# Part of an output product multiplied in a job of its own, loads paced earlier, and a new written-out order, in a fused attention and maxout kernel

## The chip, the cores and the metric

The kernel runs on one core of a Trainium2 chip. The metric is device time in microseconds, from launch to the last store, median of several executions. Before the change it is 358.24 us (three runs: 357.92, 358.24, 360.69).

## The reference: what is computed

Attention with pooled queries (batch 8, 8 heads, 1152 keys, head size 64), then a maxout layer on its output. Cut to what matters:

```python
q_pool = q.reshape(B, H, S // 2, 2, D).mean(axis=3)          # 576 queries
scores = matmul(q_pool, k.transpose(0, 1, 3, 2)) / sqrt(D)
attn = exp(scores - max); attn /= sum(attn)
x = matmul(attn, v)  ->  (4608 tokens, 512 channels)
g = maximum(x @ w1, x @ w2)                                   # 1024 wide
out = g @ w_out                                               # (4608, 512)
```

## The kernel before

**The algebra.** The maximum is split: with wd = w1 - w2, g @ w_out = max(x @ wd, 0) @ w_out + x @ (w2 @ w_out). The product w2 @ w_out (called w21) is made once. So for each block of tokens there are two kinds of matmul jobs: an h job makes two of the eight feature tiles of max(x @ wd, 0) for one stretch of tokens (stretches in `HCUTS`), and a p job makes 256 tokens of the output from twelve contraction tiles: four channel tiles of x against w21 and eight feature tiles of g against w_out.

**Attention.** Heads are taken in 32 pairs, two heads in the two row halves of TensorE. The scores of a pair are 9 key tiles by 576 queries, laid out as one long row and cut into groups of 512 columns without regard to pair borders: 324 groups. A group is multiplied (L302, letter S), then ScalarE takes the exponential of 2 x 512 columns out of PSUM (L317, letter E; where the exponential buffer turns over a group is done in two, so there are 336 E). The exponentials are then weights of the product with v (L621 and L636, letter A), normalized on VectorE (letter a), transposed into the token-major xT (by DMA, letter x, or on TensorE, letter X) and used by h and p jobs.

**Feeding a pair.** Loads of q, k and v (letter l) go through SP's DMA queue. POOL pools and casts q (L435), casts k (L405) and v (L445); letters q, k, v. From pair 5 on k is transposed by a DMA (L475, letter t) and q by eight VectorE transposes of 32 partitions (L485, letter r). Scores of a pair need both.

**The order.** Nothing is scheduled at run time. A string is read letter by letter, and each letter appends one operation to its engine's queue. Every engine runs its queue in order and waits on semaphores for what it reads or overwrites; only the waits that are needed are emitted. The letters that matter here, beside those above: 0, 1, 2, 3 are four lanes in which jobs of the weights' kind are open (w makes w21, h and p as above; the order in which jobs are opened is the string `MOE`); each digit is one unit, two matmuls in the two row halves. 4, 5, 6, 7 empty the finished job of a lane on VectorE, 8, 9, + and - do so on ScalarE. d is a difference for wd, c a cast of a weight, o a store. `BANKS` says which of the eight PSUM banks each opened job or score group takes (a p job takes two, a "wide" bank). Counting the letters E ahead of a place gives its position in the stream of exponentials; positions in this document are such counts.

**The pace of loads.** A load is issued when its buffer is free and, from a certain E on, when the exponential two before the last one ordered so far has been done:

```python
def pace():
    g = done[0] - PACE
    return [f"E{g}"] if PACE and g >= PACE_FROM else []
```

Before that E the queue issues loads as soon as a buffer is free, ahead of the place of the letter.

**The output stage.** A finished p job is copied from PSUM into `osb2`, four rows of 512 values a partition, and stored from there. p job n uses rows 0 and 1 or 2 and 3, in turn.

Of the kernel before, what the change touches and what calls it, by code (L numbers as in the profile page):

```python
# [7 lines left out]
P = 128  # L8
# [4 lines left out]
ALU = mybir.AluOpType  # L13
# [103 lines left out]
def bass_funnel_attn__then__act_maxout2_kernel(  # L117
# [11 lines left out]
    E = moe_w_out.shape[1]  # L129
# [9 lines left out]
    NC_ = C // P  # L139
    NF = F // P  # L140
# [21 lines left out]
    FILL = 28  # L162
    FILLS = 16
    PACE = 2
    PACE_FROM = 40
    FOUR = 1
    LOADS = (
# [14 lines left out]
    )  # L182
    MOE = (
        "wwhhhhpphhhhpphhhhhhhhpphhhhpphhhhphhhhpphhhhphhhhphhhhpphhhhhhhhhphphh"
    )
    BANKS = (
        "0124605424023623462032424660232342630240624702402064202420472042646264246024604640164604264126402406"
        "0240260240246304260346204040640606062061262062062402740264062402406402640642704260202402402406401640"
        "6460462056204620462046042164206204620620426026402602602602604604614646046046024604604204620420642040"
        "6406406742064264264206520640260462620620162062046206240620206204230642042042424126426046046045620642"  # L190
        "6024062046206206206206412640246056046206404024024026423236042642042626260262626426454526420642064206"
        "2454"
    )

    ctx = ExitStack()
    with ctx:
# [51 lines left out]
        def rows(half):  # L248
            return slice(half * HP, half * HP + HP)
# [273 lines left out]
        def evac_op(eng, fn, r, w, cost, after=(), alt=None):  # L523
            return dict(eng=eng, fn=fn, r=r, w=w, cost=cost, after=after, alt=alt)
# [263 lines left out]
        def p_sides(j, n, z):  # L788
            if j < NC_:
                return xT[z, j, n:n + P], w21[z, j, :]  # L790
            c = n % RING
            return gT[z, j - NC_, c:c + P], wo[z, j - NC_, :]

        def p_job(n):
            lo = n * 2 * P
            o = n % 2 * 2

            def part(j, turn):
                def go(e, m):
                    for k in range(2):  # L800
                        z = rows(turn ^ k)
                        lhs, rhs = p_sides(j, lo + k * P, z)
                        last = e.matmul(fb[m + k][:, :], lhs, rhs, start=(turn == 0 and j == 0),  # L803
                                        stop=(turn == 1 and j == NC_ + NF - 1))
                    return last
                return p_reads(j, lo, lo + 2 * P), 0.216, "s", turn == 1 and j == 0, go

            def dve(e, m):
                return e.tensor_copy(osb2[:, o:o + 2, :], wide[m // 2][:, :, :])  # L809

            def act(e, m):
                return e.copy(osb2[:, o:o + 2, :], wide[m // 2][:, :, :])

            return Job(("p", n), 2, [part(j, turn) for turn in range(2) for j in range(NC_ + NF)],
                       [evac_op("DVE", dve, [], [f"osb{o}", f"osb{o + 1}"], 0.16 + 2 * E / 960.0,
                                alt=(act, 2 * E / 1200.0))])

        def spot(n):
            b, at = divmod(n, SQ)
# [73 lines left out]
        h_at, p_at, w_at = iter(hs), iter(ps), iter(ws)  # L893
        moe = [next({"h": h_at, "p": p_at, "w": w_at}[c]) for c in MOE]
        assert next(h_at, None) is None and next(p_at, None) is None
        dve_line = {"w": [lambda n=n: cast_k0(n) for n in range(len(K0_ENG)) if K0_ENG[n] == "DVE"],
                    "y": [lambda: cast_q0(0, 0, 4), lambda: cast_q0(0, 4, QU), lambda: cast_q0(1, 0, QU)],
# [59 lines left out]
                 "m": ("Z", 0), "4": ("0", 0), "5": ("1", 0), "6": ("2", 0), "7": ("3", 0),  # L957
                 "8": ("0", 1), "9": ("1", 1), "+": ("2", 1), "-": ("3", 1)}
        for c in (
            "luFFlulllfyKQklgfbSkKEFlgFKSgESyFFlKEFgQSbESlFkSFEFFKlEySFSgESlqFFEFQlSbEFkSQElbKvSEgSlESceAAEATcESA"  # L960
            "EAhlkSaSEaASclEKAEglSAEcSAElvSaTaEhElTcSAESlAhAEScAElSSAcEAAlAqESa0a00aE0la0ScAE0SldQEaa00bSd0lEXSj0"
            "00ESvTl0h0E00eS4SlEAAkAEAlSa1ad1E1S1SEl1q1S1E1Kl1g1qE1S1SE1lQkrAEbArSdtAErArSE11avlEa1S5AElSdArESSrA"
            "dArEArSAEkAlaAaSEaAdatAESaXadjXEjSjSEXq0jl00jE0S0qr0E0lSr01rE11e41Sl1E1Sk1r10Er005St0ESv00r0ESSr0rvE"
            "lA4AAEASqalSaEAArAErAlSrSEEaAeaAArxAErSSaAEaAklrAAErS1at1ak1E1r0Sr0xE0r0Sr11E1rS1r0E050Sl0E0q0SrS0tE"
            "r01r10Er0eS0r0E0r0Skr0lE0r1S0r0E0rlSv0r1E14S11El1S1oSE1oAAEASAkEAaAlaSAEtAvSa1aE1SxS11ES111E1111ES11"
            "l1ESq5AAEAlSrSoEAroArAESrkSArEAaAalAEAaAaSvaaEtaSSrXEqArAjAEAjSrle00Ea0aS0rSE0lr0vSr0E1r01rlE114S11E"
            "1S1rSEA5AlvAEASr0E0ta0Eva0SrSE00xe00SE4AAkAESSlAEAaAaAEAlSa1aE1Sx000E0Sk11E0lS11E11S50qlE00tS00ESer0"
            "0rSE00rS0rE00r00Er0l0qSrSE0r01l1r0E14S11E1l1SroSE1r1o11roSErAoArAtEkArAAaaAArq1ESaa1E1Sx001r001E1r0S"
            "1rE0l001rS141E1rS1r1ES5AAEvAAroSSrvoESAlAAEvAaAaAlEAaAkaSa000SaEt0a000011114Ee111S111115E1S111Xl5EvS"
            "j00j0ESl0qSE0000SEl4AAAEArSSaEAaArAlqEArS1a1taE11rSESrE1e1xrS1r1EA5AAEASla0kaE0Sr00rSEq0l0r0SEr0ArAl"  # L970
            "E4SAAESr11aE1a1Srx1ESr11r1SEt5qAAAEArSe0aE0a0Slr0SEkr0S0r0E0lrS0r0E0r0Sl0rE0000ES0S0Er0tArAEArArS0aE"
            "0aq0Srx10Er1S14k1E1S11EroS1rSo1E1oAAoEvAAS1vElSAAlEAvAaSa1ESalAaAAEASa1aE1taS1rXvE1rS1j11Ej1eSrl11rE"
            "11qrSS5EAlAAkEAroS0a0oEa0S0rS0ErAAlAEASa0a0E0l0S4x00E0qSE0r00E0trSA4eAEAArS1a1Ea1k1Sr11ESr1lSr1E5AAA"
            "lEArS1a1Ea11Srx00E10S1l1E1S500tE0Sq0rS0Er00r0e0ESr00rSEl0kr00r0E0rS0l0ES00SE0A4AAEAAaAoaAoASaoSqaE11"
            "x11SESkr11t1rE11rE11rE1SrS1E1r11r1SEr11S1E1S11E1A5AEvAASoSvESlAAoAEvAaAaAElAaAa0Sa0a0E0taS00r0000E04"
            "e0Sx000r0E11141vS1x1E11r100500Sr11qE1Sr01lr110E1rS050E0Sl0r0E0SS0l0E0S0r0EArAArEAArlAkaAaArSE0etEa0a"
            "S0r0SE0rxS0rq0EA4AAEASkao1aE11o1SSE11lS11EA5AAElASa1aE1Sx0r00E0rS1rt0E0er0Sr0E1S4111ESl1r0q0E500S0lE"
            "0SrS0r0EA4lAAEAAAaaAASa1aESlk1Sx1r1ES1r11Ert11r11Er1qSSr1E1rArAEvAS1E11klS11El11vS1E1S1lvA5ESAAEAoAa"
            "oSaSESaAtaArAEArq00Ea0aSa00rExSv0r00ErS0xe0r0E0rSSr0kl0E0S00E0Sl00E0S00El0A4AEAAAaoSaSEoArAtArE00Ea0"
            "0aeS00rxE1111r00qS411E1111151S1k1E1r1Sl00500ESr000SrEl0A4AAEArSla1aE1S1S1EAAAEAlSa1aE1tSrS1rq1E1r1x1"  # L980
            "1rESSre11Er11rSk1Elr11S1E11Sl1E1A5AAEASaoSaEAoAAoEAoSa0a0tEq00rSESr0E00rx00k040E0AArvAArSrSvElArArAE"
            "AvaAaAAaAaSaSaE00a001x14E11S11E1x11Sv511E100S1SE0r1t11r0ES0500E0eSr00Er00SrSE0r00r0SEr0S00E0S00E0004"
            "0E00S0E0oS00oSE4AAAEAAaAaAeAAaEAaAAxAaAaAASa0aES0x00SE1000E0S411E1S11E111500S0E00S11E1S11E1S10E50S00"
            "E0S10E0Se10E00S00E0S00E0S00E10S41E11S11EoS11o1E1oSSo1E1AAEAAAaAaAAAaAaAxAAAAAaAaAAaAa1a1a1a11X1j11j1"
            "11111900001111111150000111o080110091o110000008101110191101000018111009101110000080101111191100000001"
            "001111910000000011111111110001000800110000o008001o11o00010181111Z9ZZZZZoZZoZZZZZZmZZZZzzZZZZZZZZZZmZ"
            "ZZZZZZzZzmzz"
        ):
            step(c)
        plan.solve()  # L990
# [51 lines left out]
```

## Time and profile before

| what | value |
|---|---|
| median of three runs | 358.24 us (357.92 to 360.69) |
| profiled execution | 358.12 us, span 356.4 us |
| TensorE busy (modelled) | 346.0 us, 6178 matmuls |
| ScalarE busy | 313.8 us, of it exponentials 302.4 |
| VectorE busy | 230.1 us |
| POOL busy | 151.4 us |
| DMA queue of SP | 83.15 MB, 87.5% of 16 engines' span |
| HBM | 62.91 MB read, 9.44 MB written |
| granted TensorE clock | 0.999 |

How to read it: busy times are unions of the instructions' spans in one profiled execution. Matmuls are pipelined and their ends are modelled, so a TensorE that is shown busy may still be waiting within a run; its weight loads (PEld) show such waits better. Idle time in front of an instruction is given with what ended it. The chain that ended last is followed back from the last instruction. Idle time of an engine that isn't the bound costs nothing by itself.

### The profile page before, as it was taken

Reading aid. Unit: us, or ns where it says so; the run is one execution under the profiler, and the core shown is the slowest. Engines: PE = TensorE matmul, PEld = TensorE weight load, DVE = VectorE, ACT = ScalarE, POOL = GpSimd, SP = SyncE. Lnnn points to the kernel's source line nnn. Section 1 sums busy time; section 2 is a strip of 40 time slices with the busy share of each in tenths; the row PEclk is TensorE's granted clock in tenths of the full one; section 3 lists DMA queues with packets and bytes.
Section 4 is the critical chain, followed back from the end, with each engine's and each line's share of the span. In section 5 each row is a group of like instructions: output and inputs, shape, how many; then the busy total and the mean of one; then the engine's idle time right before and its main releaser. Section 6 shows DMA issues by size and latency. Waiting matters only on the chain.

```text
span 356.4 us, 13757 instructions
## 1 busy us (share of the span) xinstructions
PE 346.0 (97%) x6178; PEld 218.5 (61%) x6178; DVE 230.1 (65%) x472; ACT 313.8 (88%) x354; POOL 151.4 (42%) x136
## 2 busy tenths in 40 slices
PE   7889999999899999999999999999999999999996
PEld 5556665656564675656666576556576757448753
DVE  2587589974966867985887677785586875414001
ACT  5999999999999899999999989989999796992431
POOL 2625997554564264355544455227444621010000
PEclk9999999999999999999999999999999999999999
DMA  8999999999989989998999699998999943012215
GB/s 271 403 397 398 370 255 309 280 289 261 293 252 279 315 196 350 237 301 183 278 320 260 153 230 301 237 314 234 224 299 255 267 68 75 17 32 47 61 31 148
DMA packets 76699, 84.55 MB, mean 237 GB/s; under 512 B 48480, under 2 KB 49760, under 8 KB 76640
## 3 DMA queue, kind: packets, MB, share of 16 engines
q1 hardware_dynamic: 75856, 83.15, 87.5%
q8 instruction: 48, 0.79, 0.9%
q10 hardware_dynamic: 784, 0.52, 0.5%
q14 instruction: 11, 0.09, 0.1%
HBM read 62.91 MB, written 9.44 MB: 203 GB/s over the span
## 4 chain that ended last, share of the span: by engine, by line
PE 87%; ACT 9%; DMA 2%; issue 1%; SPq 0%; DVE 0%
PE ps L803 25%; PE ps L621 20%; PE ps L302 19%; PE ps L760 16%; ACT et L317 9%; PE ps L636 3%; PE ps L593 2%; DMA qraw<-in_q_dram 2%; PE ps L846 1%; PE ps L552 0%; PE ps L533 0%; SPq L346 0%; DVE qp L428 0%; SPq L358 0%; PE ps L730 0%
## 5 line engine op out<-in xcount | busy, mean ns | idle before, releaser
L317 ACT ACTIVATE et<-ps 128x1024 bf16<-128x1024 f32 (+1 forms) x336 | 302.4, 1019 | 14.5 <-PE ps L302 9.7
L302 PE MATMUL ps<-qpT,kT 64*128 64x256 bf16 (+7 forms) x1162 | 117.3, 283 | 2.7 <-issue 1.1
L485 DVE STREAM_TRANSPOSE qpT<-qp 32x288 bf16<-32x288 bf16 x216 | 101.4, 469 | 10.4 <-PE ps L302 6.1
L760 PE MATMUL ps<-xT,wd 64*128 64x512 bf16 (+3 forms) x832 | 81.2, 311 | 0.2
L302 PEld LDWEIGHTS ps<-qpT,kT 64*128 64x128 bf16 x1162 | 48.3, 94 | 49.7 <-ACT et L317 11.3
L803 PE MATMUL ps<-wo,stage 64*128 64x512 bf16 x544 | 76.4, 376 | 0.0
L435 POOL TENSOR_TENSOR qp<-qraw 128x576 bf16<-128x576 f32 x30 | 42.1, 1406 | 61.1 <-DMA qraw<-in_q_dram 57.3
L621 PEld LDWEIGHTS ps<-vE,et 128*128 128x128 bf16 x1728 | 54.9, 97 | 13.9 <-ACT et L317 9.3
L621 PE MATMUL ps<-vE,et 128*128 128x65 bf16 x1728 | 60.7, 193 | 0.7 <-issue 0.3
L771 DVE TENSOR_SCALAR stage<-ps 128x1024 bf16<-128x1024 f32 (+3 forms) x41 | 39.7, 970 | 21.1 <-PE ps L760 20.6
L760 PEld LDWEIGHTS ps<-xT,wd 64*128 64x128 bf16 x832 | 35.6, 94 | 22.2 <-PE ps L760 1.9
L405 POOL TENSOR_SCALAR kbf<-kraw 128x1152 bf16<-128x1152 f32 x31 | 35.7, 1153 | 26.3 <-DMA kraw<-in_k_dram 25.6
L803 PE MATMUL ps<-w,xT 64*128 64x512 bf16 x272 | 40.8, 377 | 0.0
L803 PEld LDWEIGHTS ps<-wo,stage 64*128 64x128 bf16 x544 | 26.4, 94 | 20.5
L445 POOL TENSOR_SCALAR vE<-vraw 128x1152 bf16<-128x1152 f32 x24 | 27.4, 1154 | 19.4 <-PE ps L636 10.8
L809 DVE COPY stage<-ps 128x1024 f32<-128x1024 f32 x14 | 17.1, 1224 | 23.1 <-PE ps L803 23.0
L468 POOL TENSOR_SCALAR stage<-et 128x1152 bf16<-128x1152 bf16 x14 | 16.1, 1152 | 35.5 <-ACT et L317 35.5
L654 DVE TENSOR_TENSOR xnat<-ps,rc 128x256 bf16<-128x256 f32 (+2 forms) x71 | 27.6, 397 | 2.0
L651 DVE RECIPROCAL rc<-ps 128x4 f32<-128x4 f32 (+2 forms) x64 | 11.6, 182 | 25.9 <-PE ps L621 25.5
L621 PEld LDWEIGHTS ps<-stage,et 128*128 128x128 bf16 x576 | 18.1, 97 | 2.7 <-issue 2.6
L621 PE MATMUL ps<-stage,et 128*128 128x65 bf16 x576 | 19.7, 193 | 0.0
L803 PEld LDWEIGHTS ps<-w,xT 64*128 64x128 bf16 x272 | 12.5, 94 | 8.8 <-DVE stage L771 0.2
(55 smaller groups left out, 155.4 us busy)
## 6 DMA issues: line engine op xcount, KB each, us to landing
vraw<-in_v_dram SPq DMA_DIRECT2D x32, 576.0 KB, 6.1
kraw<-in_k_dram SPq DMA_DIRECT2D x31, 576.0 KB, 6.7
qraw<-in_q_dram SPq DMA_DIRECT2D x31, 576.0 KB, 6.3
out_dram<-stage SPq DMA_DIRECT2D x24, 256.0 KB, 4.1
out_dram<-stage SPq DMA_DIRECT2D x21, 128.0 KB, 3.4
xT<-in_moe_w_dram SPq DMA_DIRECT2D x4, 512.0 KB, 12.2
stage<-in_moe_w_out_dram SPq DMA_DIRECT2D x4, 512.0 KB, 14.1
stage<-in_moe_w_dram SPq DMA_DIRECT2D x4, 512.0 KB, 13.2
```

The lines of the kernel that those rows point to most:

```text
L302: last = e.matmul(ps[:, h, col:col + hi - lo], kT[i % 3][rows(h), t, :], qpT[i % 3][rows(h), lo:hi], start=True, stop=True)
L317: op("ACT", lambda e: e.activation(et2[:, :, c:c + z - a], ps[:, :, a - g * W:z - g * W], EXP, scale=scale), r=[f"b{m}", f"b{m + 1}"], w=w ...
L405: op("POOL", lambda g: g.tensor_scalar(kbf[s][:, :, :, :].rearrange("p t h d -> p h t d"), kraw[r][:, :, :, :], 1.0, 1.0, ALU.mult, ALU.mu ...
L435: op("POOL", lambda g: g.tensor_tensor(qpf[s][:, :, :], qraw[r][:, :, 0, :], qraw[r][:, :, 1, :], ALU.add), r=[f"qraw{r}"], w=[f"qp{s}.0", ...
L445: return g.tensor_scalar(vE[r][:, :, :, 0:D].rearrange("p t h d -> p h t d"), vraw[s][:, :, :, :], 1.0, 1.0, ALU.mult, ALU.mult)
L485: op("DVE", lambda e: e.transpose(view[dst:dst + 32, :, 32 * pb:32 * pb + 32], qpf[s][src:src + 32, :, 32 * db:32 * db + 32]), r=[f"qp{s}. ...
L621: last = e.matmul(fb[m][:, at * 66:at * 66 + 65], et[:, a:a + P], vE[vs][:, t, half, 0:65], start=(t == 0), stop=(t == NT - 1))
L654: todo.append(evac_op("DVE", lambda e, m, z=z, at=at, num=num, dst=dst: e.tensor_tensor(dst, a(m)[z, at:at + num, 0:D], rc[k][z, at:at + n ...
L760: last = e.matmul(fb[m + k][:, 0:size], wd[z, ct, (f0 + k) * P:(f0 + k + 1) * P], xT[z, ct, n0:n1], start=(turn == 0 and ct == 0), stop=(t ...
L771: return e.tensor_scalar_max(gT[:, f0:f0 + 2, g0:g0 + size], wide[m // 2][:, :, 0:size], 0.0)
L803: last = e.matmul(fb[m + k][:, :], lhs, rhs, start=(turn == 0 and j == 0), stop=(turn == 1 and j == NC_ + NF - 1))
L809: return e.tensor_copy(osb2[:, o:o + 2, :], wide[m // 2][:, :, :])
```

## The change

Four things are edited.

1. A new kind of job, r (`pre_job`), for the first two p jobs (tokens 0 to 511): it multiplies the first `PRE = 2` of the twelve contraction tiles, both of them channel tiles, and its result is put into the rows of `osb2` which the p job will use. p jobs 0 and 1 then run over the other ten tiles, and their evacuation on VectorE adds the PSUM to what is in `osb2`. An r job is 4 units, and p jobs 0 and 1 have 20 units where they had 24.
2. `PACE_FROM` goes from 40 to 6, so loads are held to the pace from the ninth E on.
3. The sequence of `LOADS` is changed from q 7 on, and that of the differences for wd.
4. The order string, `MOE` and `BANKS` are new; jobs are spread over four lanes instead of two until late. The letters ahead of about 28 us are nearly the same.

The diff, with the long strings cut to the lines in which p jobs 0 and 1 stand:

```diff
-    W_DIFFS = ((3, 0), (3, 1), (1, 0), (2, 0), (2, 1), (0, 0), (0, 1), (1, 1))
+    W_DIFFS = ((2, 0), (1, 1), (2, 1), (1, 0), (0, 1), (3, 0), (0, 0), (3, 1))
...
-    PACE_FROM = 40
+    PACE_FROM = 6
...
-        ("k", 5), ("v", 3), ("w", 1, 0), ("k", 6), ("q", 6), ("q", 7), ("k", 7), ("v", 4), ("v", 5),
+        ("k", 5), ("v", 3), ("w", 1, 0), ("k", 6), ("q", 6), ("k", 7), ("q", 7), ("v", 4), ("v", 5),
...
-        ("v", 12), ("q", 13), ("v", 13), ("k", 15), ("q", 14), ("v", 14), ("k", 16), ("v", 15),
-        ("q", 15), ("q", 16), ("v", 16), ("q", 17), ("k", 17), ("v", 17), ("q", 18), ("k", 18),
...
+        ("q", 13), ("v", 12), ("q", 14), ("k", 15), ("k", 16), ("v", 13), ("q", 15), ("v", 14),
+        ("v", 15), ("k", 17), ("q", 16), ("q", 17), ("q", 18), ("k", 18), ("v", 16), ("v", 17),
...
     MOE = (
-        "wwhhhhpphhhhpphhhhhhhhpphhhhpphhhhphhhhpphhhhphhhhphhhhpphhhhhhhhhphphh"
+        "wwhhhhrprphhhhpphhhhhhhhpphhhhpphhhphhhhhpphhhhphhhhphhhphphhhhhhhhphhphh"
     )
+    PRE = 2
...
-        def p_job(n):
+        def pre_job(n):
+
             lo = n * 2 * P
             o = n % 2 * 2
 
...
                         last = e.matmul(fb[m + k][:, :], lhs, rhs, start=(turn == 0 and j == 0),
+                                        stop=(turn == 1 and j == PRE - 1))
+                    return last
+                return p_reads(j, lo, lo + 2 * P), 0.216, "s", turn == 1 and j == 0, go
+
+            def dve(e, m):
+                return e.tensor_copy(osb2[:, o:o + 2, :], wide[m // 2][:, :, :])
+
+            def act(e, m):
+                return e.copy(osb2[:, o:o + 2, :], wide[m // 2][:, :, :])
+
+            return Job(("r", n), 2, [part(j, turn) for turn in range(2) for j in range(PRE)],
+                       [evac_op("DVE", dve, [], [f"pre{n}"], 0.16 + 2 * E / 960.0,
+                                alt=(act, 2 * E / 1200.0))])
+
+        def p_job(n):
+            lo = n * 2 * P
+            o = n % 2 * 2
+            first_j = PRE if n < 2 else 0
+
...
             def dve(e, m):
+                if first_j:
+                    return e.tensor_tensor(osb2[:, o:o + 2, :], wide[m // 2][:, :, :], osb2[:, o:o + 2, :], ALU.add)
                 return e.tensor_copy(osb2[:, o:o + 2, :], wide[m // 2][:, :, :])
...
-            return Job(("p", n), 2, [part(j, turn) for turn in range(2) for j in range(NC_ + NF)],
-                       [evac_op("DVE", dve, [], [f"osb{o}", f"osb{o + 1}"], 0.16 + 2 * E / 960.0,
-                                alt=(act, 2 * E / 1200.0))])
+            return Job(("p", n), 2, [part(j, turn) for turn in range(2) for j in range(first_j, NC_ + NF)],
+                       [evac_op("DVE", dve, [f"pre{n}"] if first_j else [], [f"osb{o}", f"osb{o + 1}"],
+                                0.16 + 2 * E / 960.0, alt=None if first_j else (act, 2 * E / 1200.0))])
...
-            "lA4AAEASqalSaEAArAErAlSrSEEaAeaAArxAErSSaAEaAklrAAErS1at1ak1E1r0Sr0xE0r0Sr11E1rS1r0E050Sl0E0q0SrS0tE"
...
+            "AAAElArSrSEArAAaaAESaSaEltAEerAArAESqaSrAElrAAaAkESa1a11Er2t2rS2kE216S11E11qS53El33S33Er3SrS3E3r330E"
...
```

The rest of the order strings can't be shown at length; what the prediction says of places in them is counted from them letter by letter.

More of the change, by code (lines that the diff above doesn't have):

```diff
@@ L812, in act, with part, go @@
                 return e.copy(osb2[:, o:o + 2, :], wide[m // 2][:, :, :])
-            return Job(("p", n), 2, [part(j, turn) for turn in range(2) for j in range(NC_ + NF)],
-                       [evac_op("DVE", dve, [], [f"osb{o}", f"osb{o + 1}"], 0.16 + 2 * E / 960.0,
+            return Job(("r", n), 2, [part(j, turn) for turn in range(2) for j in range(PRE)],
+                       [evac_op("DVE", dve, [], [f"pre{n}"], 0.16 + 2 * E / 960.0,
                                 alt=(act, 2 * E / 1200.0))])
+        def p_job(n):
+            lo = n * 2 * P
+            o = n % 2 * 2
+            first_j = PRE if n < 2 else 0
+            def part(j, turn):
+                def go(e, m):
+                    for k in range(2):
+                        z = rows(turn ^ k)
+                        lhs, rhs = p_sides(j, lo + k * P, z)
+                        last = e.matmul(fb[m + k][:, :], lhs, rhs, start=(turn == 0 and j == first_j),
+                                        stop=(turn == 1 and j == NC_ + NF - 1))
+                    return last
+                return p_reads(j, lo, lo + 2 * P), 0.216, "s", turn == 1 and j == first_j, go
+            def dve(e, m):
[7 more added lines that the diff above has]
+                                0.16 + 2 * E / 960.0, alt=None if first_j else (act, 2 * E / 1200.0))])
         def spot(n):
@@ L892, in bass_funnel_attn__then__act_maxout2_kernel @@
         ws = [w_job(c) for c in W_PAIRS]
-        h_at, p_at, w_at = iter(hs), iter(ps), iter(ws)
-        moe = [next({"h": h_at, "p": p_at, "w": w_at}[c]) for c in MOE]
+        rs = [pre_job(n) for n in range(2 if PRE else 0)]
+        h_at, p_at, w_at, r_at = iter(hs), iter(ps), iter(ws), iter(rs)
+        moe = [next({"h": h_at, "p": p_at, "w": w_at, "r": r_at}[c]) for c in MOE]
         assert next(h_at, None) is None and next(p_at, None) is None
@@ L965, in bass_funnel_attn__then__act_maxout2_kernel @@
[L965 to L974, printed above, removed]
@@ L988, in bass_funnel_attn__then__act_maxout2_kernel @@
+            "AEAAaAaAeAAaEAaAkArArAAatAaSaSaE00ro00rSEo10rl00lEr0Sr1x1E41S11E1x13532S3xE33S22E2oS2o2E2oS2o3E633S3"
+            "E3S330E0eS33E3Sv33E30Sv3E3S333E3S700E00S0oE0S0o00EoSS00EAAAEAAaAaAAAaAaAxAAAAoAaAaAAaAa0a0a0a00X0j00"
+            "j0011118233331111222353332222o07000+111o103333000224221111005003333007022221+111332222018133222233+3"
+            "311-000000000001111222203222330030003111111103321+1111090307000oZ8ZoZZoZZoZZZoZZZZZZZmZZZZZzzZZZZZZZ"
+            "mZZZZZZZzZzmzz"
         ):
```

52 lines of the change are left out of this document (28 added, 24 removed), and 10 rows, old and new, of the table LOADS.

## The prediction

> **What bounds the kernel now.** I read the totals and the chain first, then the stages, then the groups and the waits of the engine that the stages point to.
>
> The page's totals and its chain that ended last:
>
> ```profile
> PE 346.0 (97%) x6178; PEld 218.5 (61%) x6178; DVE 230.1 (65%) x472; ACT 313.8 (88%) x354; POOL 151.4 (42%) x136
> PE 87%; ACT 9%; DMA 2%; issue 1%; SPq 0%; DVE 0%
> ```
>
> TensorE looks like the only bound. But a busy PE is modelled, so I cut the span where the work changes: start, the stretches that the chain gives to ScalarE, the body, and what follows the last exponential (stage, its length, then busy time of PE, PEld, DVE, ACT, POOL with counts, clock, DMA share, GB/s).
>
> ```profile
> 9.40:44.70 35.30, 32.49 (x686) 20.17 (x688) 24.00 (x40) 34.84 (x39) 22.03 (x20) 1.00 1.02 391
> 44.70:60.00 15.30, 14.89 (x254) 8.27 (x252) 13.38 (x29) 15.29 (x18) 14.02 (x12) 1.00 1.16 282
> 60.00:121.00 61.00, 59.74 (x1040) 37.35 (x1041) 45.40 (x95) 60.00 (x68) 31.41 (x27) 1.00 1.05 285
> 121.00:322.00 201.00, 200.72 (x3595) 126.23 (x3591) 139.54 (x288) 189.36 (x210) 82.14 (x69) 1.00 0.91 220
> 322.00:353.30 31.30, 31.23 (x524) 21.22 (x520) 4.74 (x15) 9.37 (x15) 0.00 (x0) 1.00 0.26 62
> 353.30:356.40 3.10, 0.00 (x0) 0.00 (x0) 0.26 (x1) 0.00 (x0) 0.00 (x0) 0.90 0.40 114
> ```
>
> Up to 121 us ScalarE is as full as TensorE; from 121 to 322 it idles 201.00 - 189.36 = 11.6 us; after 322 it has little to do and TensorE runs alone for 31.3 us, with 3.1 us of the last store behind it. So the time is a sum of three: the end of the exponentials (322.0), the TensorE tail (31.3), the store (3.1), together 356.4. The profiled execution took 358.12 us, 1.7 more than its span, and the median of the runs is 358.24; the sum is made against 358.12.
>
> The group of the exponentials, what ScalarE waited for in all, and two rows of its timeline:
>
> ```profile
> L317 ACT ACTIVATE et<-ps 128x1024 bf16<-128x1024 f32 (+1 forms) x336 | 302.4, 1019 | 14.5 <-PE ps L302 9.7
> ACT et L317 <- PE ps L302: 9.7, 15, 2.1
> ACT et L317 <- PE ps L621: 2.9, 3, 1.1
> 237.25 10.21 ACT L317 ACTIVATE et<-ps 128x1024 bf16<-128x1024 f32 x11 [1.07 <-PE ps L302]
> 314.46 7.51 ACT L317 ACTIVATE et<-ps 128x1024 bf16<-128x1024 f32 x8
> ```
>
> 302.4 us over 336 instructions is 0.90 us for one E of the order: that is the step in which I count below. The last E ends at 314.46 + 7.51 = 322.0. Idle before an E sums to 14.5 us, nearly all of it waiting for scores or for matmuls of L621. A change can thus gain by closing those waits, or by having less TensorE work behind the last E; it loses if scores come later.
>
> **The change part by part.** Positions are counted in the order strings of both kernels: the number of E ahead of a letter.
>
> *The work multiplied ahead.* Two r jobs of 8 matmuls (2 tiles x 2 turns x 2 blocks) leave p jobs 0 and 1, which lose 8 each. Rows for a run of 36 attention matmuls and one of eight of L803 (of the chain in order of time), the copy that empties p, and the stage in which p 0 and p 1 stand:
>
> ```profile
> 61.94 1.20 PE ps L621 x36
> 73.63 0.86 PE ps L803 x8
> L809 DVE COPY stage<-ps 128x1024 f32<-128x1024 f32 x14 | 17.1, 1224 | 23.1 <-PE ps L803 23.0
> 70.00:80.00 10.00, 10.00 (x129) 5.35 (x125) 7.84 (x14) 10.00 (x12) 5.68 (x5) 1.00 1.01 274
> 44.70 13.43 ACT et L317 x15
> ```
>
> The number of matmuls is the same: 2 x 0.86 = 1.7 us of TensorE is moved, not removed. It would be worth 1.7 us if it went where the chain runs through ScalarE (44.70 to 58.13, about steps 43 to 57), since TensorE has room there. In the new order it does not: r 0 stands at steps 69 to 70 with p 0 from 71, r 1 at 74 to 77 with p 1 from 79, while before p 0 began at 69 and p 1 at 74. It comes straight ahead of the job from which it was cut, in the same stretch. I counted every unit of TensorE ahead of each E, at 0.215 us for two matmuls of L803, L760 or a score group (less for narrower ones) and 0.30 for nine of L621, the same in both orders: from E 30 on they are never more than 0.45 us apart, equal at 221 of 306 places, and 31.9 against 31.6 us behind the last E, a shift that the body gets back as +0.3. So the move itself gives 0.
>
> It adds two evacuations of 1.22 us on VectorE, 2.45 us in a stretch where it is 7.84 of 10 us busy; the two p evacuations become additions of equal width. VectorE's room of 2.2 us there hides most. What waits behind: p 0 takes bank 2, which r 0 just filled, and stands only two score groups and five pairs of matmuls behind it, 7 x 0.215 = 1.5 us against an evacuation of 1.22. Between 0 and two whole evacuations (2.4 us), in the likeliest case covered; I take 0. Below nothing it can't go, since no work leaves.
>
> *ScalarE as evacuator.* The old order has no evacuation on ScalarE ahead of the last E; the new one has one, of h job (6, 6), at step 249. The copies to ScalarE behind the last E fall from 14 to 9, and VectorE, 4.74 of 31.3 us busy there, takes them. A whole-width evacuation of that kind is seen only as a copy:
>
> ```profile
> L812 ACT COPY stage<-ps 128x1024 f32<-128x1024 f32 x3 | 3.0, 1012 | 12.1 <-PE ps L803 12.1
> ```
>
> So up to 1.0 us in the stream of E. At this very place the row at 237.25 shows ScalarE waiting 1.07 us for scores (the E there has 249 others ahead of it). If the wait stays, the copy fills it: 0; if it goes, 1.0. I take +0.3.
>
> *Loads paced from E 6, not 40.* Until now the queue ran ahead (two issue groups with size and median landing, then the queue's and POOL's timeline, then a stage):
>
> ```profile
> stage<-in_moe_w_dram SPq DMA_DIRECT2D x4, 512.0 KB, 13.2
> qraw<-in_q_dram SPq DMA_DIRECT2D x31, 576.0 KB, 6.3
> 23.96 4.05 SPq L358 DMA_DIRECT2D qraw<-in_q_dram  x2
> 28.05 0.52 SPq L346 DMA_DIRECT2D kraw<-in_k_dram  x1
> 29.16 1.41 POOL L435 TENSOR_TENSOR qp<-qraw 128x576 bf16<-128x576 f32 x1 [4.35 <-DMA qraw<-in_q_dram]
> 31.79 2.49 POOL L506 TENSOR_TENSOR wd<-stage,xT 128x512 bf16<-128x512 f32 x2 [1.22 <-DMA stage<-in_moe_w_dram]
> 40.00:50.00 10.00, 9.99 (x224) 6.53 (x220) 7.49 (x16) 9.97 (x13) 10.00 (x10) 1.00 1.01 302
> ```
>
> The load of k 5 (letter at step 35) was issued at 28 us, when some 23 E were done. Under the new pace each load waits for an E two back, so 22 loads of about 0.55 MB go out over steps 9 to 40, 31 x 0.90 = 28 us: 12 MB in 28 us is 430 GB/s, against the 391 GB/s that the queues moved from 9.4 to 44.7. The bytes arrive at the same rate, each a little behind need. POOL is where it bites: it is full from 40 to 50 us, and a difference that waits 2 us longer for w1 delays the casts of pairs 5 and 6 and the first h job at step 52 by as much. Price 0 to 2 us, nothing below, since no E waited for a load there; ScalarE was full, with scores one to two steps ahead, so I take 0.
>
> *The order searched anew.* This is the large part. For pairs 5 to 31, I counted how many steps the last of the eight VectorE transposes of q stands ahead of the pair's first score group. Before: median 13, two pairs at 3 or less, none at 1 or less. After: median 3, fourteen at 3 or less, seven at 1 or less (6, 11, 14, 15, 20, 22, 29). The DMA transposes of k stood 10 to 22 steps ahead and now stand 7 to 21; the loads of v move up to 35 steps later, yet from pair 10 on still 7 or more ahead of their casts. The rows that price this are those of the k transposes and their landings, of a pair that had only 2 steps before (pair 6), and of one whose cast waited for its load (pair 10):
>
> ```profile
> kT<-kbf SPq DMA_TRANSPOSE x27, 5.5
> DMA to landing us min/median/max: 3.2/5.5/7.5
> 58.56 1.44 DVE L485 STREAM_TRANSPOSE qpT<-qp 32x288 bf16<-32x288 bf16 x3
> 61.33 0.61 PE L302 MATMUL ps<-qpT,kT 64*128 64x320 bf16 x8
> 86.28 1.42 POOL L435 TENSOR_TENSOR qp<-qraw 128x576 bf16<-128x576 f32 x1 [5.00 <-DMA qraw<-in_q_dram]
> ```
>
> Pair 6's last transpose ended at 60.00 and its scores came inside the run from 61.33, with no idle time noted: 2 steps were enough. The loads of q land in 6.3 us, and POOL's wait of 5.00 shows that their casts already follow at once, without harm. The shortest k lead, 7 steps, is 6.3 us against landings of at most 7.5. So most pairs should still just make it; if one does not, TensorE stands in front of its scores, and every matmul behind them in the queue with it. The order gains nothing where nothing waited before: the waits for scores in the body came of TensorE's own sequence, which is the same. From below, a gain is not excluded: fewer of 11.6 us of waits. I take +0.4 for a few late pairs.
>
> The sum: 358.1 + 0 + 0.3 + 0 + 0.4 = **358.8 us**. About 1% (3.6 us) is what a measurement of this kernel tells from no change.
>
> The Trainium skill speaks against the pacing: "DMA: Bandwidth & Descriptors", Rules for kernel authors, says to issue a DMA early, compute meanwhile and wait for it late, so that its fixed cost is overlapped. By that rule the shortened leads would end as in the first rival, 361.9 to 365.2, instead of 358.8. The trace of before agrees in so far as POOL waited for landings while TensorE did not; no run here shows it yet with short leads.
>
> **The rivals.**
> *Late queries (slower).* One mechanism: the last q transposes end after the place of the pair's first scores, TensorE stands, and ScalarE behind it. For it: fourteen leads of 3 steps or less, and a VectorE queue in which evacuations of 1.22 us stand between transposes. Against: pair 6 above. One transpose:
>
> ```profile
> L485 DVE STREAM_TRANSPOSE qpT<-qp 32x288 bf16<-32x288 bf16 x216 | 101.4, 469 | 10.4 <-PE ps L302 6.1
> ```
>
> Seven pairs late by one transpose cost 7 x 0.47 = 3.3 us, fourteen 6.6: 361.9 to 365.2. It decides from a lateness of more than 1.4 us, the one to two steps by which scores lead. Chance 0.25.
>
> *The waits close (faster).* If the new banks and four lanes let TensorE run further ahead, half to all of the 11.6 us goes: 346.5 to 352.3, a smaller share 354. Against: equal TensorE work ahead of every E. The one place that is not work:
>
> ```profile
> PE ps L302 <- issue: 1.1, 1, 1.1
> ```
>
> It may go by chance. Chance 0.10.
>
> *The move does what its words suggest:* 1.7 us gained, 356.4 to 357. The position of r speaks against it. Chance 0.05, inside 1%. My forecast keeps 0.60 (its own range 357 to 361).
>
> **How the numbers follow.** The range is to leave out at most 2 in 10: I cut the faster rival below 355.5 (about 0.09 of chance) and the slower one above 365 (about 0.08). Faster by over 1%: the second rival, 0.10. Slower by over 1%: the first, 0.25. Within: the rest, 0.65.
>
> **What would show it.** Right: the last exponential ends near 322 to 323, idle time of L317 stays 13 to 16 us, the tail keeps 31 us, one more group of two VectorE copies of 128x1024, and the p 0 and p 1 evacuations as tensor-tensor near 1.2 us. The late-query rival would show as TensorE or its weight loads waiting for L485 or for kT, and an L317 idle time of 18 us or more, with POOL's waits for qraw or for w1 grown between 25 and 50 us. The faster one would show L317 idle under 9 us. I would be wrong altogether if the tail changed by more than 1 us, or if E instructions themselves took longer than 0.90 us a step.

## The result and the profile after

The changed kernel takes 361.5 us in the median of 22 runs, the kernel before 358.81 in the median of 22 beside them: a ratio of 1.0075, with a 95% interval of 1.0056 to 1.0094. That is 2.7 us or 0.75% slower: inside the 1% that I called no change, with an interval that leaves 1 out. The profiled execution took 361.93 us (span 360.0), against 358.12 (span 356.4) before, so its own loss of 3.8 us overstates that of the medians by about one. The ratios leave out executions more than 1.5% above the fastest of their kernel (three of these 22), so here and below a ratio need not be the quotient of two medians.

The totals and the chain of the kernel after:

```profile
PE 346.9 (96%) x6177; PEld 219.8 (61%) x6178; DVE 234.2 (65%) x478; ACT 313.1 (87%) x350; POOL 150.8 (42%) x136
PE 81%; ACT 7%; DMA 5%; POOL 3%; DVE 2%; issue 1%; SPq 0%
```

The work is the same within a microsecond on TensorE. New in the chain are 3% of POOL and 5% of DMA: before, POOL did not stand in it and DMA had 2%. The stages of after (stage, length, busy time of PE, PEld, DVE, ACT, POOL with counts, clock, DMA share, GB/s):

```profile
9.40:44.70 35.30, 31.40 (x677) 19.76 (x676) 22.37 (x36) 34.15 (x39) 18.67 (x17) 1.00 1.02 389
44.70:60.00 15.30, 13.58 (x244) 7.87 (x240) 13.11 (x29) 14.16 (x17) 14.83 (x14) 1.00 0.96 228
60.00:121.00 61.00, 59.27 (x984) 35.71 (x980) 46.24 (x93) 58.39 (x66) 28.16 (x24) 0.97 1.04 254
121.00:322.00 201.00, 200.63 (x3594) 127.52 (x3592) 141.51 (x293) 190.62 (x213) 86.35 (x73) 1.00 0.92 231
```

The group of its exponentials:

```profile
L318 ACT ACTIVATE et<-ps 128x1024 bf16<-128x1024 f32 (+1 forms) x336 | 303.3, 1016 | 16.2 <-PE ps L303 11.6
```

ScalarE's wait for scores in all:

```profile
ACT et L318 <- PE ps L303: 11.6, 20, 2.1
```

The last row of E in ScalarE's timeline:

```profile
311.63 13.96 ACT L318 ACTIVATE et<-ps 128x1024 bf16<-128x1024 f32 x15 [0.52 <-PE ps L303]
```

(Lines stand one later than before: L317 is now L318.) The last E ends at 311.63 + 13.96 = 325.6 instead of 322.0, and the span ends 34.4 us behind it, as before. So the whole loss lies ahead of the last E, and the stages say where: ScalarE is 0.7 us less busy ahead of 44.7 us, 1.1 less from there to 60, 1.6 less from there to 121; behind 121 us it is 1.3 busier (190.62 against 189.36), 1.04 of it the evacuation that moved there. POOL does 17 operations in the first stage instead of 20.

Matching each E with the E of the same number in the trace of before gives the lag. It is -0.64 us at E 6 (this execution began faster), +0.20 at E 42, **+1.51 at E 48**, +1.53 at E 90, **+3.77 at E 102** and +3.69 at the last. Two short places hold 3.5 us of it; the other 0.8 came between E 6 and E 42, most of it between E 20 and E 36.

**Place 1, E 43 to 48.** ScalarE's timeline of before, then of after (start, length):

```profile
39.48 23.35 ACT L317 ACTIVATE et<-ps 128x1024 bf16<-128x1024 f32 x26
```

```profile
39.80 8.47 ACT L318 ACTIVATE et<-ps 128x1024 bf16<-128x1024 f32 x10
49.41 12.98 ACT L318 ACTIVATE et<-ps 128x1024 bf16<-128x1024 f32 x14 [1.14 <-PE ps L303]
```

One unbroken run has become two with 1.14 us between. TensorE's wait of that moment:

```profile
PE ps L637 <- POOL stage L446: 1.2, 1, 1.2
```

POOL's timeline of after, and the difference ahead of the same cast before:

```profile
34.36 1.16 POOL L446 TENSOR_SCALAR vE<-vraw 128x1152 bf16<-128x1152 f32 x1 [3.27 <-DMA vraw<-in_v_dram]
45.68 1.27 POOL L507 TENSOR_TENSOR wd<-stage,xT 128x512 bf16<-128x512 f32 x1
46.99 1.15 POOL L446 TENSOR_SCALAR stage<-vraw 128x1152 bf16<-128x1152 f32 x1
```

```profile
43.32 1.27 POOL L506 TENSOR_TENSOR wd<-stage,xT 128x512 bf16<-128x512 f32 x1
```

SP's issues of the loads of q 3 and k 4 before, and the cast of v 3; then the same two issues after:

```profile
16.77 2.17 SPq L358 DMA_DIRECT2D qraw<-in_q_dram  x1
22.85 0.55 SPq L346 DMA_DIRECT2D kraw<-in_k_dram  x1
44.62 1.15 POOL L445 TENSOR_SCALAR stage<-vraw 128x1152 bf16<-128x1152 f32 x1
```

```profile
23.62 0.34 SPq L359 DMA_DIRECT2D qraw<-in_q_dram  x1
30.36 0.37 SPq L347 DMA_DIRECT2D kraw<-in_k_dram  x1
```

The value product of pair 3 (L637) stood until v 3 was cast, at 46.99 instead of 44.62. A difference stands directly ahead of that cast in both orders (45.68 after, 43.32 before). What differs is what POOL does a little earlier: in the new order it stands idle for 3.27 us until v 2 is there, casts it at 34.36 and makes its differences behind it, where the old order made two of them ahead of v 2 (31.79 to 34.28); and the pace issues the early loads some 7 us later. The experiments part the two. A smaller wait of the same kind stands earlier, on the transposes of q 3 (L534; the first pairs' q is transposed by TensorE):

```profile
PE ps L534 <- POOL qp L436: 0.5, 1, 0.5
```

**Place 2, E 94 to 102.** ScalarE of before, then of after:

```profile
93.13 19.61 ACT L317 ACTIVATE et<-ps 128x1024 bf16<-128x1024 f32 x22 [0.49 <-PE ps L302]
```

```profile
94.51 2.85 ACT L318 ACTIVATE et<-ps 128x1024 bf16<-128x1024 f32 x3 [1.39 <-PE ps L303]
97.89 1.02 ACT L318 ACTIVATE et<-ps 128x1024 bf16<-128x1024 f32 x1 [0.53 <-PE ps L303]
99.17 2.87 ACT L318 ACTIVATE et<-ps 128x1024 bf16<-128x1024 f32 x3 [0.26 <-PE ps L303]
```

TensorE's weight loads at that place, of before and then of after:

```profile
92.70 0.33 PEld L302 LDWEIGHTS ps<-qpT,kT 64*128 64x128 bf16 x7 [1.38 <-issue]
```

```profile
94.11 0.17 PEld L303 LDWEIGHTS ps<-qpT,kT 64*128 64x128 bf16 x5 [1.46 <-issue]
```

The stage behind them, of before and then of after:

```profile
96.20:99.60 3.40, 3.40 (x40) 1.49 (x36) 3.15 (x6) 3.40 (x4) 0.55 (x2) 1.00 1.02 348
```

```profile
96.20:99.60 3.40, 3.40 (x38) 2.16 (x36) 2.14 (x6) 2.61 (x4) 1.53 (x2) 0.50 0.98 287
```

In both kernels TensorE waits here for nothing that the profile can name ("issue"). The wait costs after 0.75 us more than before (the lag is +2.28 at E 96). After, its clock is then granted at 0.50 for 3.4 us: half of that, 1.7 us of matmuls, is lost by estimate, and ScalarE's gaps follow (the lag grows by 1.49 to E 102). The low clock does not make the loss of the medians: 5 of the 22 runs of after have a mean clock of 0.994 or 0.995, the profiled one among them, and the other 17 have a median near 361.3. Whether the new order makes it likelier is open: 4 of the 70 runs of before that stand beside the experiments have such a clock.

**The new job and the moved evacuation.** Groups of after:

```profile
L805 PE MATMUL ps<-w,xT 64*128 64x512 bf16 x16 | 2.6, 379 | 0.0
L811 DVE COPY stage<-ps 128x1024 f32<-128x1024 f32 x2 | 2.5, 1225 | 3.2 <-PE ps L805 3.2
L837 DVE TENSOR_TENSOR stage<-ps,stage 128x1024 f32<-128x1024 f32 x2 | 2.5, 1225 | 1.1 <-PE ps L830 1.1
```

ScalarE's timeline of after at the place of h job (6, 6):

```profile
239.63 1.04 ACT L776 ACTIVATE stage<-ps 128x1024 bf16<-128x1024 f32 x1
240.83 4.69 ACT L318 ACTIVATE et<-ps 128x1024 bf16<-128x1024 f32 x5 [0.16 <-PE ps L303]
```

The r jobs are there, with two more copies of 1225 ns and two additions that take the same. The lag does not move between E 48 and E 90, where they stand. ScalarE's evacuation of 1.04 us stands where before there was a wait of 1.07.

### The profile page after: what moved, and what is told of

The parts are those of the page before. It is cut to its first block, busy times and chain, and to the rows that moved or that the text cites. A ratio compares the mean times of both kernels' runs of the same rounds, so it can differ in the third digit from the quotient of the medians.

```text
span 360.0 us, 13720 instructions
## 1 busy us (share of the span) xinstructions
PE 346.9 (96%) x6177; PEld 219.8 (61%) x6178; DVE 234.2 (65%) x478; ACT 313.1 (87%) x350; POOL 150.8 (42%) x136
## 4 chain that ended last, share of the span: by engine, by line
PE 81%; ACT 7%; DMA 5%; POOL 3%; DVE 2%; issue 1%; SPq 0%
PE ps L830 23%; PE ps L622 18%; PE ps L303 18%; PE ps L761 18%; ACT et L318 7%; DMA kraw<-in_k_dram 3%; PE ps L637 2%; DMA xT<-in_moe_w_dram 2%; PE ps L875 1%; POOL wd L507 1%; POOL qp L436 1%; DVE xT L499 1%; POOL kbf L406 1%; PE ps L805 0%; POOL stage L446 0%
## 5 line engine op out<-in xcount | busy, mean ns | idle before, releaser
L318 ACT ACTIVATE et<-ps 128x1024 bf16<-128x1024 f32 (+1 forms) x336 | 303.3, 1016 | 16.2 <-PE ps L303 11.6
L303 PE MATMUL ps<-qpT,kT 64*128 64x256 bf16 (+7 forms) x1162 | 113.9, 284 | 4.1 <-ACT et L318 2.0
L761 PE MATMUL ps<-xT,wd 64*128 64x512 bf16 (+3 forms) x832 | 79.8, 313 | 0.3
L830 PE MATMUL ps<-wo,stage 64*128 64x512 bf16 x544 | 73.1, 376 | 0.0
L772 DVE TENSOR_SCALAR stage<-ps 128x1024 bf16<-128x1024 f32 (+3 forms) x45 | 41.4, 921 | 36.4 <-PE ps L761 35.7
L830 PE MATMUL ps<-w,xT 64*128 64x512 bf16 x256 | 36.5, 376 | 0.0
L838 DVE COPY stage<-ps 128x1024 f32<-128x1024 f32 x12 | 14.7, 1224 | 18.8 <-PE ps L830 18.8
L469 POOL TENSOR_SCALAR rem<-et 128x1152 bf16<-128x1152 bf16 x9 | 10.3, 1150 | 17.2 <-ACT et L318 17.2
```

What stands on the lines that cost most here:

```text
L303: last = e.matmul(ps[:, h, col:col + hi - lo], kT[i % 3][rows(h), t, :], qpT[i % 3][rows(h), lo:hi], start=True, stop=True)
L318: op("ACT", lambda e: e.activation(et2[:, :, c:c + z - a], ps[:, :, a - g * W:z - g * W], EXP, scale=scale), r=[f"b{m}", f"b{m + 1}"], w=w ...
L469: op("POOL", lambda g: g.tensor_scalar(rems[s][:, :, :, :], src, 1.0, 1.0, ALU.mult, ALU.mult), r=[f"et{i % 2}.{g - first(i)}" for g in ra ...
L761: last = e.matmul(fb[m + k][:, 0:size], wd[z, ct, (f0 + k) * P:(f0 + k + 1) * P], xT[z, ct, n0:n1], start=(turn == 0 and ct == 0), stop=(t ...
L772: return e.tensor_scalar_max(gT[:, f0:f0 + 2, g0:g0 + size], wide[m // 2][:, :, 0:size], 0.0)
```

## The experiments

The theory after this reading: the pace costs, through POOL; the new order costs, through v 3; the r jobs are neutral. The rival: the short leads of the new order (queries, and values cast late) cost small amounts all through the body. All ratios are against the kernel before, run on the same chip.

**Pace undone in after.**

```diff
-    PACE_FROM = 6
+    PACE_FROM = 40
```

> The changed kernel with its pace of loads put back to E 40; nothing else. Pacing theory (loads held from E 6 make POOL late, +1.5 us by the 48th E): 1.5 us less than the changed kernel, ratio to before about 1.003, and the 48th E again within 0.3 us of before. Late-query theory (the new order's short leads cost the time): no change, ratio 1.0075. Extra-job theory: no change.

Measured: 359.85 us, ratio 1.0041 [1.0015, 1.0066]. Against 1.0075 that is 0.0034, or 1.2 us (the two intervals overlap a little). Its profile had +0.61 of lag at E 48, more than the 0.3 expected, and -0.14 at E 96 (before's unnamed wait at 92 us is missing here), and then lost 1.9 us in one place that I had not expected. POOL, TensorE and ScalarE of this kernel there:

```profile
234.79 1.15 POOL L406 TENSOR_SCALAR kbf<-kraw 128x1152 bf16<-128x1152 f32 x1 [3.18 <-DMA kraw<-in_k_dram]
235.91 1.15 POOL L446 TENSOR_SCALAR vE<-vraw 128x1152 bf16<-128x1152 f32 x1
237.21 2.33 PE L622 MATMUL ps<-vE,et 128*128 128x65 bf16 x72 [1.90 <-POOL vE L446]
239.90 5.61 ACT L318 ACTIVATE et<-ps 128x1024 bf16<-128x1024 f32 x6 [2.10 <-PE ps L303]
```

The cast of v of pair 22 stood in POOL's queue behind a cast of k that waited 3.18 us for its load; TensorE waited 1.90 for v. So the order can lose time by late values, in single executions. The early place is there too, POOL's timeline of this kernel:

```profile
33.51 1.15 POOL L446 TENSOR_SCALAR vE<-vraw 128x1152 bf16<-128x1152 f32 x1 [2.74 <-DMA vraw<-in_v_dram]
46.10 1.14 POOL L446 TENSOR_SCALAR stage<-vraw 128x1152 bf16<-128x1152 f32 x1
```

Without the pace POOL still waits 2.74 us for v 2 and casts v 3 at 46.10: of the 2.37 us by which after is late there, 1.5 are the order's and 0.9 the pace's.

**Pace brought into before.**

```diff
-    PACE_FROM = 40
+    PACE_FROM = 6
```

> The kernel before with the pace of loads from E 6; nothing else. Pacing theory: 1 to 2 us more than before, ratio 1.003 to 1.006, the loss visible by the 48th E. Late-query and extra-job theory: ratio 1.000 within 0.002, since order and jobs are those of before.

Measured: 359.72, ratio 1.0024 [1.0002, 1.0046], or +0.9 us. The pace costs about the same in either order. POOL's timeline of this kernel:

```profile
31.07 1.40 POOL L435 TENSOR_TENSOR qp<-qraw 128x576 bf16<-128x576 f32 x1 [5.87 <-DMA qraw<-in_q_dram]
```

TensorE's waits of this kernel from 25 to 38 us:

```profile
PE ps L621 <- issue: 1.0, 1, 1.0
```

The cast of q 3 came at 31.07 instead of 29.16: the load was issued about 7 us later and came 1.9 us later. But in the old order TensorE does not stand for it, since its transposes come later in the queue. What its profile lost there is an unnamed wait of 1.0 us (0.3 before), of the kind that the last section traces to TensorE's own instructions, so where the 0.9 us of the median go in the old order is not shown. Nor is it shown whether the pace acts by such waits too: one of over 0.5 us stands at this place in three of the five profiles with the pace from E 6 and in two of the seven others.

**The r jobs undone in after.** Its units go back to p 0 and p 1, in the same places of the order string; two evacuations fall out.

```diff
-        "wwhhhhrprphhhhpphhhhhhhhpp...
+        "wwhhhhpphhhhpphhhhhhhhpp...
-    PRE = 2
+    PRE = 0
-  ...1a11Er2t2rS2kE216S11E11qS53E...
+  ...1a11Er3t3rS3kE31S11E11qS53E...
```

> The changed kernel with p jobs 0 and 1 whole again: the r jobs' units are the first four of the p job, which opens where r opened, and the two added evacuations are gone. Extra-job theory (two evacuations and a bank held cost time): 1 to 2.4 us less than the changed kernel, ratio 1.001 to 1.005. Pacing and late-query theory: no change, ratio 1.0075 within 0.002.

Measured: 361.56, ratio 1.0084 [1.0056, 1.0113], as after. The r jobs are not seen to cost or to gain; the intervals leave room for about 1.2 us either way. Its profile has the first place again and more of it (TensorE's waits, from 25 to 38 us and from 38 to 60):

```profile
PE ps L534 <- POOL qp L436: 1.0, 1, 1.0
PE ps L637 <- POOL stage L446: 1.4, 1, 1.4
```

Its lag is +2.67 at E 48 and +2.38 at the last E: all lost by E 48. The same two waits, longest of each in us, over the profiles of all kernels with the new order ahead of 50 us and v 3 behind the difference (the last three are described below):

| kernel | pace from | L534 for q 3 | L637 for v 3 |
|---|---|---|---|
| after | E 6 | 0.5 | 1.2 |
| r jobs undone | E 6 | 1.0 | 1.4 |
| fewer filling matmuls | E 6 | 1.0 | 1.2 |
| pace undone | E 40 | none | 0.7 |
| values earlier | E 40 | none | 0.7 |
| values and loads earlier | E 40 | none | 0.5 |
| r jobs earlier (its start was 1.2 us late) | E 40 | none | none |

In these profiles the pace is the first column altogether and about 0.6 us of the second: 1.1 to 1.6 us, next to the 1.2 of the times.

**Fewer filling matmuls at the start**, to move TensorE's instruction count against its data.

```diff
-    FILL = 28
+    FILL = 12
```

> The changed kernel with 12 instead of 28 warming matmuls at its start, 32 TensorE records fewer ahead of everything else. It tells what the wait near 93 us is, that names no releaser. If TensorE's instructions come late there, the wait stays at the same count of TensorE records (about 3266) and so moves 32 records further on in the work, or goes. If it is a wait for data of pair 9, it stays in front of the same scores. Time within 1 us of the changed kernel, unless that wait and a lowered clock behind it go, then up to 2 us less.

Measured: 363.1, ratio 1.0117 [1.0090, 1.0143], 1.5 us above after, where at most 1 was expected. Its profile starts late (lag +0.89 at E 6), but so do two profiles of kernels with all 28 (r jobs earlier +1.25, v 3 first with pace 40 +0.98), so it is not shown that the fewer matmuls cost this. In these three the trace records the full clock only from 10.5 to 13.7 us on, in the other nine from 4.0 to 6.2. The unnamed wait stayed, but in front of other work (weight loads, TensorE):

```profile
96.65 0.09 PEld L553 LDWEIGHTS ps<-ident,xnat 64*128 64x128 bf16 x1 [0.76 <-issue]
```

Counted from the start over matmuls and weight loads together, it stands at TensorE's record 3266 before, 3265 after and 3265 here: 32 records were taken out ahead of it and it moved 32 records on in the work. So it belongs to the number of the instruction, not to scores of pair 9 or to their data.

**Values earlier** (with pace 40): the casts of v from pair 10 on up to 12 steps earlier; and **values and loads earlier**: loads from step 100 on up to 5 steps earlier as well. Letters of the order string moved, the first of them:

```diff
-  ...ASa3aE3t3E3eSSlE333k3SE7A...
+  ...ASa3aEv3t3E3eSSlE333k3SE7A...
```

> The changed kernel with the pace back at E 40 and, from pair 10 on, the POOL casts of v up to 12 steps earlier in the order (not closer than 8 steps to their load). The profile with the pace at 40 alone showed TensorE standing 1.9 us for the cast of v of pair 22, which was queued behind a late cast of k. Late-value theory (the short leads of the v casts cost what pacing does not): 0.7 to 1.5 us less than with the pace at 40 alone (ratio 1.0041), so 1.000 to 1.002, and no wait of L622 for POOL. Other theory (instructions fetched late, or short q leads): no change, 1.003 to 1.005.

> As the run with the v casts earlier, and from step 100 on every load of q, k and v up to 5 steps earlier too, as far as the buffer is free. If loads that land late are what remains (POOL waits for kraw and qraw, and its later casts with it): 0.5 us or more less than with the v casts alone, at or under before (ratio 0.998 to 1.001). If it isn't the loads: the same as with the v casts alone.

Measured: 361.16, ratio 1.0052 [1.0022, 1.0081]; and 362.05, ratio 1.0095 [1.0059, 1.0131]. Neither is better than 1.0041. So late values are not seen to be what the body loses by on the whole, although the profile of pace 40 showed one such wait. Why the earlier loads came out worse is open: the profile of that kernel shows no single place, but five unnamed waits of 0.5 to 1.3 us, 3.7 us together, next to a lag of +4.13 at its last E; all five are of the kind that the last section describes.

**Values later in before**: its casts and loads of v from pair 10 on put at the steps that the new order has.

```diff
-  ..."1S1rSEA5AlvAEASr0E0ta0Eva0SrSE00xe00SE4...
+  ..."1S1rSEA5AlAEASr0E0ta0Ea0SrSE00xe00SE4...
```

> The kernel before with the loads and POOL casts of v, from pair 10 on, put off to the places that they have in the new order; all else as before, the pace too. Late-value theory: 0.7 to 1.5 us more than before, ratio 1.002 to 1.004, with TensorE waiting for POOL in the profile of some executions. Other theory: ratio 1.000 within 0.002.

Measured: 359.49, ratio 1.0028 [1.0000, 1.0055]. Inconclusive: about 1 us of cost, with an interval from 0 to 2, but its profile (span 356.3) has no wait of TensorE for POOL.

**r jobs where the chain ran through ScalarE** (with pace 40): their units at steps 56 and 64 to 65, with banks of their own, some 15 steps ahead of their p jobs.

```diff
-        "wwhhhhrprphhhhpp...
+        "wwhhrhrhpphhhhpp...
-  ...Slq36E3S33E3kS700E...AESaSaEltAEerAA...
+  ...Slq36E22223S33E63kS700E...AESaSaE000ltAE04erAA...
```

> The changed kernel with the pace at 40 and the two r jobs at steps 56 and 64 to 65, ahead of the stretch where p 0 and p 1 stand, in banks that are free there. If 1.7 us of TensorE work, moved to where ScalarE is the bound, is worth its length: 1.7 us less than with the pace at 40 alone, ratio 0.999. If it is worth nothing, because every later E still waits for its own work and the tail is unchanged: the same, 1.003 to 1.005.

Measured: 363.31, ratio 1.0133 [1.0093, 1.0172], 3.3 us more than pace 40 alone. TensorE and ScalarE of this kernel at the two places:

```profile
58.29 1.28 PE L805 MATMUL ps<-w,xT 64*128 64x512 bf16 x8 [0.89 <-DVE stage L772]
60.04 1.94 ACT L318 ACTIVATE et<-ps 128x1024 bf16<-128x1024 f32 x2 [1.55 <-PE ps L303]
70.70 4.69 ACT L318 ACTIVATE et<-ps 128x1024 bf16<-128x1024 f32 x5 [1.74 <-PE ps L303]
```

The first r waited 0.89 us for its bank to be emptied, and 1.28 us of matmuls then stood ahead of the next scores. The lag rises from +1.24 at E 54 to +5.25 at E 66, and nothing comes back where p 0 and p 1 lack these matmuls: it is +5.12 at E 90.

**v 3 cast ahead of the difference**, one POOL operation earlier, with pace 6 and with pace 40.

```diff
-  ...AESrEd1t1r1ESr1Av5ESEda...
+  ...AESrEvd1t1r1ESr1A5ESEda...
```

> The changed kernel (pace from E 6) with one POOL operation moved: the cast of v of pair 3 goes ahead of the difference for wd that stood just before it, 1.27 us. In every profile of the new order TensorE (L637) waits 0.9 to 1.6 us for this cast, in those of the old order 0 to 0.2. If that wait is where the early loss enters: 1 to 1.3 us less than the changed kernel, ratio 1.004, no wait of L637 for POOL, the 48th E within 0.5 us of before. If POOL is merely late as a whole and the next thing waits instead (the first h job, or q of pair 5): no change, 1.0075.

> The same move with the pace at 40. If the wait for the cast is what is left of the early loss in the new order: 0.5 to 0.9 us less than with the pace at 40 alone (1.0041), so 1.0015 to 1.003. If what is left comes of single late instructions and loads in the body: no change, 1.004.

Measured: 360.09, ratio 1.0054 [1.0026, 1.0082]; and 359.24, ratio 1.0023 [0.9998, 1.0048]. With pace 6, POOL's timeline of this kernel:

```profile
46.23 1.16 POOL L446 TENSOR_SCALAR stage<-vraw 128x1152 bf16<-128x1152 f32 x1
```

TensorE's wait from 25 to 38 us:

```profile
PE ps L534 <- POOL qp L436: 0.6, 1, 0.6
```

The wait of L637 is gone in both kernels, and the time falls by 0.0021 and 0.0018 (0.75 and 0.65 us): nearly the same in both, though each difference alone is within the intervals. The step between the two, which is the pace once more, is 0.0031, next to 0.0034 and 0.0024 above. With pace 6 the wait for q 3 is still there; with pace 40 there is none. With pace 40 the profile loses nothing more up to E 48 (lag +0.98 at E 6, +1.00 at E 48). With pace 6 the 48th E was expected within 0.5 us of before and came 1.34 late: this execution also had the wait for q 3 and an unnamed wait of 1.1 us at 29.8 us.

With pace and v 3 both put right, 0.0023 is left, 0.8 us, which may be nothing. None of the kernels beats the one before.

## Why the prediction was right or wrong

Read as a chain of ratios, 1.0075 is 0.0034 of pace, 0.0018 of v 3 and 0.0023 that is left: 1.2 + 0.65 + 0.8 = 2.7 us, with nothing for the r jobs. The intervals of the steps overlap; the pace and the r jobs are each tested in a kernel that changes them alone. The forecast of no change beyond 1% held, but 358.8 was 2.7 us short of the median of after: a term taken as 0 measured 1.2, and one taken as +0.4 measured 1.5. That the two together stay under 1% is luck, not something that the sum had seen.

- **"The move itself gives 0": right, as far as the intervals tell.** Undoing it gave 1.0084 against 1.0075. Its aside, that the matmuls "would be worth 1.7 us" where the chain runs through ScalarE, "since TensorE has room there", was wrong at the places tried: it cost 3.3 us. The row of before for that stage had TensorE busy 14.89 of 15.30 us: ScalarE being the chain did not mean that TensorE had room for a block of 1.3 us ahead of scores. Other places, or r cut into smaller pieces, were not tried.
- **Two evacuations, "0 to 2.4, I take 0": right.** Two copies of 1225 ns came, the additions cost as much as copies, and the lag stayed flat around them.
- **ScalarE's evacuation, +0.3: about 0.** It filled the wait.
- **Loads paced, "0 to 2 us, I take 0": a mis-sized term.** It measured 0.9 in the old order and 1.2 in the new. The failing sentence is "since no E waited for a load there; ScalarE was full, with scores one to two steps ahead, so I take 0". The bytes did arrive at the same rate (389 GB/s against 391), and the place was right ("POOL is where it bites"), but the victims were not the casts of pairs 5 and 6 nor the first h job: they were the casts of q 3 and v 3, whose readers on TensorE come directly behind them in the new order. I had looked at the loads from k 5 on, and at what POOL waits for, not at how much later TensorE reads what POOL makes.
- **The new order, +0.4 "for a few late pairs": too small, and the reason wrong.** With the pace undone 1.5 us are left (1.0041; the interval is 0.5 to 2.4). Queries from pair 5 on were hardly late. This is the only entry of after that names their transposes:

```profile
PEld ps L303 <- DVE qpT L486: 0.4, 2, 0.3
```

What was found of the order's cost is one cast of v at 45 us: with the loads of before it still comes 1.5 us late, and putting it ahead of one difference gave back 0.65 to 0.75, less than the intervals can tell. The 0.8 us that are left have no place yet. I had counted how far q and k stand ahead of their scores and how far v stands behind its load, not how far v stands ahead of its product, nor what stands ahead of it in POOL's queue.

Of the rivals, **late queries** nearly has the time but not the mechanism. Its lower end was 361.9, a sum that stands on 358.6; from 358.4, the forecast without the +0.4 for late pairs, it is 361.7 to 365.0. But from E 102 (in pair 9) to the end the lag does not grow, though six of the seven shortest leads (pairs 11 to 29) lie there. By the page of the Trainium skill that I weighed ("DMA: Bandwidth & Descriptors", Rules for kernel authors: issue early, wait late) the time should be that of this rival. The trace agrees in part: loads issued 7 us later cost 0.9 to 1.2 us, early and, in the new order, through POOL, while loads moved five steps earlier in the body gained nothing (1.0095 against 1.0041). **The waits close**: no, the idle time ahead of E grew from 14.5 to 16.2 us. **The move does what its words suggest**: no.

Of the signs, the tail (34.4 us), the new copies and the additions came as written. The last E ended at 325.6, not at 322 to 323, and the idle time of 16.2 us is just past the 13 to 16 that I gave, under the 18 of the rival. The E themselves did not get slower (13.96 us for 15 in the last row, 0.93 each; before 7.51 for 8, 0.94). My forecast's own span of 357 to 361 us is missed by 0.5; of the 2.7 us by which 358.8 fell short, the pace and v 3 explain 1.9.

## What to carry to other kernels

When loads are held back, follow each one to the engine that casts it, and in that engine's queue name what stands ahead of the cast and how soon its result is read: the price is there and not in the bytes. A short lead was harmless as long as the queue that makes it was not itself behind; where an unrelated wait stood ahead in the same queue (3.18 us for a load of k), the cast behind it came too late. Work that can be done while such a wait lasts belongs ahead of it. And an engine beside the one that sets the pace has room only for what fits between the operations that feed it.

## What the runs showed of the hardware that was not expected

**TensorE can wait for its own instructions.** The unnamed wait stands at record 3265 or 3266 in eight of the twelve profiles, whatever is to be done there, 0.5 to 1.5 us long. It is one of a series: in all the profiles together 25 waits of weight loads longer than 0.45 us name no releaser, and 24 of them stand at records that are whole multiples of 256 apart, give or take one. The trace has a DMA queue that carries instructions (packets, MB, share of 16 engines; the same in before and after):

```profile
q8 instruction: 48, 0.79, 0.9%
```

Its packets are 16 KB, one for some 259 of TensorE's records. Each of the 24 waits ended 1.2 to 1.6 us (once 0.8) after one of these packets had landed. At record 3265 the packet had started 43 to 142 records ahead of the place where TensorE stood, in after with 2.81 us to land; in the four kernels without a wait it had started 156 to 177 records ahead. The Trainium skill, "Runtime: NRT & Kernel Launch", Instruction fetch mechanics, holds that such fetches are mostly hidden; here they weren't always. Why a packet comes late is open.

**The granted clock fell without a full idle stretch.** TensorE in after, ahead of the half clock:

```profile
92.00:94.00 2.00, 0.93 (x24) 0.60 (x19) 1.01 (x4) 1.12 (x2) 0.00 (x0) 1.00 0.82 93
94.00:96.00 2.00, 1.34 (x35) 1.15 (x36) 0.62 (x2) 1.49 (x2) 0.00 (x0) 1.00 0.71 198
```

It was busy 2.27 of these 4 us, and got half its clock for the next 3.4. The Trainium skill, "TensorE: Matmul & The Clock Gate", Part 1, gives one idle window of about 3.4 us as what brings the slow clock; here 1.7 us of idle time, in pieces, stood ahead of it in this execution, while before, with one wait of 1.1 us at the same place, the clock stayed at 1.00. Idle time alone does not decide it: with the pace undone TensorE was busy for 1.51 of the 3.40 us from 233.8 us on, and with v 3 first and pace 40 for 1.73 of the 3.40 from 91.7, and the clock stayed at 1.00 in both. What else it takes is open.
